# A fused attention and two-MoE kernel on one core: the second block of tokens also multiplied in 256-token pieces in its first half, attention steps spread over three quarter stages

## The chip, the core and the metric

The kernel runs on one core of a Trainium2 chip. A core has five engines that run side by side, each through its own list of instructions in order: TensorE (PE; its weight loads are shown apart as PEld), VectorE (DVE), ScalarE (ACT), GpSimd (POOL) and SyncE (SP), which issues the DMAs here. An instruction that waits holds up all that stand behind it on its engine. The metric is the device time of one execution in microseconds (us); lower is better.

## The reference

Three layers follow one another, all in float32:

```python
# 1. mLSTM attention: batch 2, 8 heads, 768 steps, head size 40
m_new = np.maximum(f_gate[:, :, t] + m, i_gate[:, :, t])
C = f_stab * C + i_stab * outer(v_t, k_t);  n = f_stab * n + i_stab * k_t
y[:, :, t] = sigmoid(o_t) * (C @ q_t) / max(|n . q_t|, 1)
# 2. first MoE: x is [1536, 320], w_in [320, 2048], w_out [2048, 320]
h = x @ w_in
g = np.where(h >= 1, h, np.where(h <= -1, 0.0, (h + 1) ** 2 / 4))
x = g @ w_out
# 3. second MoE: 8 experts, w1[e] [320, 1024], w2[e] [1024, 320]
P = exp(x @ w_gate - max), then 8 rounds of row and column scaling
out = sum over e of P[:, e] * (relu(x @ w1[e]) @ w2[e])
```

## The kernel before, in words

The 1536 tokens are worked as 12 attention tiles of 128 (tile t is chunk t // 2 of batch t % 2; the state `Cst` of a batch is carried from tile t to t + 2). The output of a tile goes, split into a high and a low part, into `XH` and `XL`, which hold all tokens and are the input of the first MoE.

Float32 accuracy is made from pieces: a product of the first MoE takes, for each of its three parts of the 320 inputs, high by high, high by low and low by high, in 8 matmuls (`gemm_k`, L124, into a bank `bk_g1`); the second product takes 8 more (`moe1_g2`, L557 to L561, into three banks `bk_g2`). Between the two stand the activation in `moe1_act`: three passes of ScalarE (L541 to L543), a maximum of VectorE (L545), a copy on ScalarE (L546, the high part) and a subtraction on VectorE (L547, the low part).

The first MoE runs in four stages of 512 tokens, by the table `STAGES` (L40): tokens 0-511 with the first half of d_ff (hf 0) in products of 256 tokens, tokens 512-1023 with both halves in products of 512, tokens 0-511 with the second half, tokens 1024-1535 with both. A bank `bk_g1` holds 512 columns: one block of d_ff for 512 tokens, or two blocks for 256. In the text a "product" is what fills one such bank; there are 8 to each half of d_ff and 512 tokens. With 256-token pieces the stage also begins with three matmuls that set the banks `bk_g2` to zero (L578), and each product with two matmuls of zeros that are overwritten (`warm`, L296). In those pieces the activation is done in place in the bank, which so stays occupied until L547.

Attention is written as a generator (`attn`) whose steps are issued between the products. A tile takes eight such steps: scores (L379) of four heads, a scan along time on VectorE (L383) that makes the decay factors, their product `A` with the scores (L385), the same for the other four heads, the read of the state (L395, into the one bank `bk_ax`), `A` times the values (L400), the state's update (L407, L440), the division and gate (L419 to L433), a transpose (L446) and the split into `XH` and `XL` (L114, L116). Tiles 0 and 1 are done before stage 0. A credit grows by `RATE` with each block of d_ff, and one step is issued for each whole credit (L609 to L620); no step is issued past tile 7 before the fourth block of the second half of stage 1 (L612), since the columns of later tokens in `XH` and `XL` are lent to the activations until then. A piece of 256 or 512 tokens starts only when its tiles are done (L592).

The weights of the first MoE come as 64-bit floats and are decoded on chip in 18 pieces (`decode`, L207 to L223: one pass of ScalarE, four of VectorE, then a split); `pump_w` issues one piece's step. Nine pieces belong to the first half of d_ff, and nine to the second, which are issued one for each product from stage 1 on.

The framework orders the instructions of each engine by their dependencies and the order in which they were issued; `tc.issue_after(x)` puts what is issued under it on the engine of x behind x in that order; it adds no semaphore wait of its own.

Of the kernel before, what the change touches and what calls it, by code (L numbers as in the profile page):

```python
# [34 lines left out]
WA, WG = 4, 2  # L35
PUMP = (0, 2, 4, 5, 6, 7, 10, 12, 13)
GP = 8
RATE = ((3.4, 0), (0, 2.25), (0, 2.25), (2, 2))

STAGES = ((0, (0,), 256), (512, (0, 1), 512), (0, (1,), 512), (1024, (0, 1), 512))  # L40
LAG1, LAG2 = 2, 3


# [5 lines left out]
def mlstm_moe_moe_kernel(  # L49
# [76 lines left out]
    with ExitStack() as atx:  # L126
# [346 lines left out]
        def pump_w():  # L473
            w_state[0] = next(wjobs, 99)
# [62 lines left out]
        dve_at = []  # L537
# [31 lines left out]

        credit = 0  # L570
        held = ap.tile([128, 3, 512], F32, name="held")
        for si, (t0, hfs, w) in enumerate(STAGES):
            nf = 512 // w
            f_last = hfs[-1] * 8 + 7
            pp = [bank("g2") for _ in range(3)]
            if w < 512:
                for p in pp:
                    mm(p, wz, wz[:, 0:1].to_broadcast([128, 512]), start=True, stop=False)  # L578
            prevs = []
            for hf in hfs:  # L580
                if si == 1 and hf == 1:
                    while w_state[0] < 18:
                        pump_w()
                    rtx.close()
                    rtx = ExitStack()
                    open_right(rtx, hp=1, raw=2, gw=1)
                    wgr = pools["gw"].tile([128, 3, NE], F32, name="wgr")
                    wgs = pools["gw"].tile([128, 5, NE], F32R, name="wgs")
                    wg2 = pools["gw"].tile([128, 2, 2, NE], F32R, name="wg2")
                    hearly[0] = -1  # L590
                for o in range(0, 512, w):
                    while len(done) * 128 < t0 + o + w:  # L592
                        next(rest)
                    for ff in range(hf * 8, hf * 8 + 8, nf):
                        need_w(ff + nf - 1)
                        pg = bank("g1")
                        if w < 512:
                            warm(WG, pg)
                        for u in range(nf):
                            fc = (ff + u) % 8 * 128  # L600
                            pe_at = gemm_k(pg[:, u * w : u * w + w], WM[hf][0], slice(fc, fc + 128), slice(t0 + o, t0 + o + w))
                        while len(prevs) >= (LAG2 if w == 512 else LAG1):
                            moe1_g2(*prevs.pop(0))
                        st = ff == hfs[0] * 8 and w == 512
                        sp = ff + nf - 1 == f_last and o + w == 512
                        prevs.append(([p[:, o : o + w] for p in pp], st, sp, ff, w, *moe1_act(pg, w < 512)))
                        if w_state[0] < (9, 18, 18, 18)[si]:
                            pump_w()
                        credit += nf * RATE[si][hf]  # L609
                        while credit >= 1:  # L610

                            if len(done) >= 8 and (si == 0 or si == 1 and ff < 8 + LAG2):  # L612
                                break
                            if si:

                                with tc.issue_after(pe_at[0].ins), tc.issue_after(dve_at[-3].ins):
                                    next(rest, None)
                            else:
                                next(rest, None)
                            credit -= 1  # L620
                        if si == 3 and ff == 11:
                            nc.sync.dma_start(wgr, w_gate)
                            split_k(wgs, 0, NE, wgr)
                            act(out=wg2.rearrange("p k u e -> p u k e"), in_=f(wgs[:, 0:4, :]).rearrange("p (u k) e -> p u k e", u=2), func=ACTF.Copy)
                            cur, jobs = expert_w(0)
                        if si == 3 and ff >= 11:
                            next(jobs, None)
                            next(jobs, None)
            for _ in jobs if si == 3 else ():
                pass  # L630
            for p in prevs:
                moe1_g2(*p)
            if si == 0:
                for k, p in enumerate(pp):
                    act(out=held[:, k, :], in_=p, func=ACTF.Copy)
                continue
            if si == 2:
                for k, p in enumerate(pp):
                    vec.tensor_tensor(out=p, in0=p, in1=held[:, k, :], op=ALU.add)
            tr = htile(512, "gs")  # L640
            act(out=tr[0:64], in_=pp[2][64:128], func=ACTF.Copy)
            act(out=tr[64:128], in_=pp[2][0:64], func=ACTF.Copy)
            vec.tensor_tensor(out=tr, in0=pp[2], in1=tr, op=ALU.add)
            split_x([(0, pp[0]), (1, pp[1]), (2, tr)], slice(t0, t0 + 512))
# [159 lines left out]
```

## Time and profile before

| | us |
|---|---|
| median of 3 runs (lowest to highest) | 995.71 (994.46 to 996.32) |
| the profiled execution: its time | 994.85 |
| the profiled execution: span from first to last instruction | 993.1 |
| stage 0 (tokens 0-511, hf 0), from PE's first product | 36.4 to about 116.5 |
| stage 1, first half (tokens 512-1023, hf 0) | 116.5 to 143.5 |
| stage 1, second half | 143.5 to 196.8 |
| stage 2 (tokens 0-511, hf 1) | 196.8 to 231.2 |
| stage 3 (tokens 1024-1535) | 231.2 to 292.4 |
| second MoE | 292.4 to 993.1 |

The start and end of a row of the timeline are microseconds from the span's start. A busy time of PE is no measure of its work, as matmuls overlap: what one costs in a stream is the distance from its start to the next one's start.

### The profile page before, as it was taken

The page shows a single profiled execution, that of the slowest core. Times are in us where ns is not written, and L with a number is a line of the kernel's source. Part 1 is how long each engine was busy: PE and PEld are TensorE (multiplying, and loading weights), DVE is VectorE, ACT ScalarE, POOL GpSimd, SP SyncE. Part 2 cuts the span into 40 slices and gives each one's busy share as a digit, 9 for nine tenths or more (in the row PEclk, how much of TensorE's full clock was granted, in tenths as well). Part 3 has the DMA queues.
Part 4 walks back from the last instruction along what each step waited for, and adds up shares of the span by engine and source line. Part 5 has one row for each costly group of instructions (what it writes and reads, how often), then busy time and mean ns, then how long its engine had stood idle before and what let it go on. Part 6 is the DMA issues. An engine that isn't in the chain of part 4 may idle for free.

```text
span 993.1 us, 13483 instructions
## 1 busy us (share of the span) xinstructions
PE 979.6 (99%) x5520; PEld 861.8 (87%) x5520; DVE 470.1 (47%) x853; ACT 344.8 (35%) x622; POOL 31.2 (3%) x43
## 2 busy tenths in 40 slices
PE   9999899999999999999999999999999999999998
PEld 5789788887878899999999999989999999999997
DVE  9999977655563644322522432242253234222222
ACT  3743684477773224211411321141132123111111
POOL 2212101000000000000000000000000000000000
PEclk9999999999999999999999999999999999999999
DMA  5865413000132002100400210030021002000000
GB/s 171 263 169 172 143 57 99 12 1 0 47 113 75 1 1 64 54 1 1 117 1 1 74 44 1 7 111 1 1 87 31 1 17 72 1 1 1 27 27 27
DMA packets 42190, 51.91 MB, mean 52 GB/s; under 512 B 3360, under 2 KB 35744, under 8 KB 42128
## 3 DMA queue, kind: packets, MB, share of 16 engines
q1 hardware_dynamic: 42128, 51.05, 17.3%
q8 instruction: 43, 0.70, 0.3%
q14 instruction: 19, 0.16, 0.0%
HBM read 49.03 MB, written 2.01 MB: 51 GB/s over the span
## 4 chain that ended last, share of the span: by engine, by line
PE 89%; DVE 5%; ACT 3%; DMA 1%; issue 1%; SPq 0%; DVEq 0%; ACTq 0%
PE bk_g L124 41%; PE bk_g L704 9%; PE bk_g L706 8%; PE bk_g L705 8%; PE bk_ax L705 3%; PE bk_ax L704 3%; PE bk_ax L706 3%; PE bk_at L400 2%; PE bk_g L296 2%; PE bk_g L559 2%; PE bk_g L558 1%; PE bk_g L557 1%; PE bk_at L379 1%; DMA raw<-in_w_dram 1%; PE bk_g L561 1%
## 5 line engine op out<-in xcount | busy, mean ns | idle before, releaser
L124 PE MATMUL bk_g<-XH,wk 128*128 128x512 f32 (+1 forms) x1240 | 399.8, 388 | 1.6 <-DVE gs L545 1.6
L724 DVE SCALAR_TENSOR_TENSOR lo<-bk_g,hi 128x512 fp32r<-128x512 f32 x192 | 132.6, 691 | 372.6 <-ACT hi L723 371.7
L124 PE MATMUL bk_g<-XL,wk 128*128 128x512 f32 (+1 forms) x744 | 285.4, 384 | 0.0
L723 ACT ACTIVATE hi<-bk_g 128x512 fp32r<-128x512 f32 x192 | 114.9, 599 | 453.2 <-PE bk_g L124 453.0
L124 PEld LDWEIGHTS bk_g<-XH,wk 128*128 128x128 f32 x1240 | 230.6, 188 | 45.1 <-DVE gs L545 2.6
L704 PE MATMUL bk_g<-wf,hi 128*128 128x320 f32 x576 | 177.4, 308 | 1.1 <-ACT hi L723 1.1
L705 PE MATMUL bk_g<-wf,hi 128*128 128x320 f32 x576 | 177.0, 307 | 0.0
L706 PE MATMUL bk_g<-wf,lo 128*128 128x320 f32 x576 | 176.9, 308 | 0.0
L124 PEld LDWEIGHTS bk_g<-XL,wk 128*128 128x128 f32 x744 | 140.0, 188 | 21.4
L704 PEld LDWEIGHTS bk_g<-wf,hi 128*128 128x128 f32 x576 | 108.0, 187 | 8.1 <-ACT hi L723 1.6
L705 PEld LDWEIGHTS bk_g<-wf,hi 128*128 128x128 f32 x576 | 108.1, 188 | 6.3
L706 PEld LDWEIGHTS bk_g<-wf,lo 128*128 128x128 f32 x576 | 107.9, 187 | 0.0
L705 PE MATMUL bk_ax<-wf,hi 128*128 128x320 f32 x192 | 59.1, 308 | 0.0
L704 PE MATMUL bk_ax<-wf,hi 128*128 128x320 f32 x192 | 59.0, 307 | 0.0
L706 PE MATMUL bk_ax<-wf,lo 128*128 128x320 f32 x192 | 58.4, 304 | 0.0
L545 DVE TENSOR_TENSOR gs<-bk_g,gs 128x512 f32<-128x512 f32 x40 | 27.5, 688 | 26.8 <-ACT gs L543 26.4
L541 ACT ACTIVATE gs<-bk_g 128x512 f32<-128x512 f32 x48 | 28.5, 594 | 28.7 <-PE bk_g L124 28.1
L738 DVE SCALAR_TENSOR_TENSOR acc<-bk_g,P,acc 128x320 f32<-128x320 f32 x63 | 30.8, 545 | 15.3 <-PE bk_g L706 15.3
L531 DVE TENSOR_TENSOR wf<-raw,wf 128x640 fp32r<-128x640 f32 x32 | 26.3, 826 | 20.7 <-ACT wf L530 20.5
L704 PEld LDWEIGHTS bk_ax<-wf,hi 128*128 128x128 f32 x192 | 36.1, 188 | 0.0
L706 PEld LDWEIGHTS bk_ax<-wf,lo 128*128 128x128 f32 x192 | 36.1, 188 | 0.0
L705 PEld LDWEIGHTS bk_ax<-wf,hi 128*128 128x128 f32 x192 | 35.9, 187 | 0.0
(198 smaller groups left out, 999.6 us busy)
## 6 DMA issues: line engine op xcount, KB each, us to landing
raw<-in_w_dram SPq DMA_DIRECT2D x32, 320.0 KB
raw<-in_w_dram SPq DMA_DIRECT2D x32, 256.0 KB
kvo_t<-in_kvo_dram SPq DMA_DIRECT2D x12, 484.0 KB
raw<-in_w_out_dram SPq DMA_DIRECT2D x8, 640.0 KB
raw<-in_w_in_dram SPq DMA_DIRECT2D x8, 512.0 KB
raw<-in_w_dram SPq DMA_DIRECT2D x64, 64.0 KB
qk<-in_qk_dram SPq DMA_DIRECT2D x24, 160.0 KB
G<-g_d SPq DMA_DIRECT2D x5, 512.0 KB
```

Of the source, the lines that this page charges most:

```text
L124: return [mm(dst, a, b, start=i == 0, stop=i == len(seq) - 1) for i, (a, b) in enumerate(seq)]
L296: mm(to, wz, wz[:, 0:1].to_broadcast([128, 512]), start=True, stop=True)
L400: mm(pa[:, h * 41 : (h + 1) * 41], A[h % 2][:, h // 2, :], vw[:, h, :], start=True, stop=True)
L531: vec.tensor_tensor(out=wf[:, fs, 320:640], in0=rs[n], in1=f(wf[:, fs, 0:320]), op=ALU.subtract)
L541: act(out=t, in_=pg, func=ACTF.Relu, scale=-1.0, bias=1.0)
L545: dve_at.append(vec.tensor_tensor(out=g, in0=pg, in1=t, op=ALU.max))
L704: mm(pp[i], hi[:, ts], wf[:, ff, 0:320], start=st, stop=False)
L705: mm(pp[i], hi[:, ts], wf[:, ff, 320:640], start=False, stop=False)
L706: mm(pp[i], lo[:, ts], wf[:, ff, 0:320], start=False, stop=sp)
L723: act(out=hi, in_=pg, func=ACTF.Relu)
L724: vec.scalar_tensor_tensor(out=lo, in0=pg, scalar=0.0, in1=f(hi), op0=ALU.max, op1=ALU.subtract)
L738: vec.scalar_tensor_tensor(out=acc[:, t, :], in0=pp[i], scalar=P[:, t, e : e + 1], in1=acc[:, t, :], op0=ALU.mult, op1=ALU.add)
```

## The change

Four edits. The table `STAGES` holds a width for each half of d_ff, and stage 1 has 256 tokens for its first half and 512 for its second. Its banks are therefore zeroed at its start (`zeroed`), and its first eight products carry the two matmuls of zeros. `RATE` gives 2.4 steps for a block in stage 0 (3.4 before) and 2.4 in the first half of stage 1 (none before). From stage 1 on, `pump_w` is issued behind the last-but-one maximum (`dve_at[-2]`). The attention steps of stage 1's first half are issued freely; those of its second half and of later stages stay behind the matmul and the maximum as before.

```diff
-RATE = ((3.4, 0), (0, 2.25), (0, 2.25), (2, 2))
-STAGES = ((0, (0,), 256), (512, (0, 1), 512), (0, (1,), 512), (1024, (0, 1), 512))
+RATE = ((2.4, 0), (2.4, 2.25), (0, 2.25), (2, 2))
+STAGES = ((0, ((0, 256),)), (512, ((0, 256), (1, 512))), (0, ((1, 512),)), (1024, ((0, 512), (1, 512))))
...
-        for si, (t0, hfs, w) in enumerate(STAGES):
-            nf = 512 // w
-            f_last = hfs[-1] * 8 + 7
+        for si, (t0, hfs) in enumerate(STAGES):
+            f_last = hfs[-1][0] * 8 + 7
+            zeroed = hfs[0][1] < 512
...
-            if w < 512:
+            if zeroed:
                 for p in pp:
                     mm(p, wz, wz[:, 0:1].to_broadcast([128, 512]), start=True, stop=False)
...
-            for hf in hfs:
+            for hf, w in hfs:
+                nf = 512 // w
...
-                        st = ff == hfs[0] * 8 and w == 512
+                        st = ff == hfs[0][0] * 8 and not zeroed
...
                         if w_state[0] < (9, 18, 18, 18)[si]:
-                            pump_w()
+                            if si:
+                                with tc.issue_after(dve_at[-2].ins):
+                                    pump_w()
+                            else:
+                                pump_w()
                         credit += nf * RATE[si][hf]
...
-                            if si:
+                            if si and hf + si > 1:
```

How the instructions of an engine stand is shown at three places. The first is PE in the first half of stage 1, for one product and the start of what follows it. Before (`bk_g1_1390` is the bank of the product, `wk_88` its weights):

```order
L124 MATMUL bk_g1_1390<-XH_66,wk_88 128x512
L124 MATMUL bk_g1_1390<-XL_67,wk_88 128x512
L124 MATMUL bk_g1_1390<-XH_66,wk_88 128x512 x2
L124 MATMUL bk_g1_1390<-XL_67,wk_88 128x512
L124 MATMUL bk_g1_1390<-XH_66,wk_88 128x512 x2
L124 MATMUL bk_g1_1390<-XL_67,wk_88 128x512
L561 MATMUL bk_g2_1268<-XL_67,wf_89 128x512
```

And in the changed kernel, from the two matmuls of zeros on (`bk_g1_1457` is the bank):

```order
L296 LDWEIGHTS wz_91
L296 MATMUL bk_g1_1457<-wz_91 128x512
L296 LDWEIGHTS wz_91
L296 MATMUL bk_g1_1457<-wz_91 128x512
L124 MATMUL bk_g1_1457<-XH_66,wk_88 128x256
L124 MATMUL bk_g1_1457<-XL_67,wk_88 128x256
L124 MATMUL bk_g1_1457<-XH_66,wk_88 128x256 x2
L124 MATMUL bk_g1_1457<-XL_67,wk_88 128x256
L124 MATMUL bk_g1_1457<-XH_66,wk_88 128x256 x2
L124 MATMUL bk_g1_1457<-XL_67,wk_88 128x256
```

Eight matmuls of 512 columns became 16 of 256, with two matmuls of zeros ahead of them.

The second place is DVE in stage 0, around the second product `A` of tile 4 (`A_752` before, `A_846` after; `G0_90` holds its decay factors, `g_all_80` those of the next tile). Before:

```order
L385 TENSOR_TENSOR A_744<-bk_at_739,G0_90 128x512
L433 TENSOR_TENSOR sg_637<-sg_637,den_717 128x320
L383 SCALAR_TENSOR_TENSOR G0_90<-G0_90,id4_116 128x512
L213 TENSOR_SCALAR dv_757<-dv_757 128x512
L385 TENSOR_TENSOR A_752<-bk_at_747,G0_90 128x512
L116 TENSOR_TENSOR XL_67<-bk_ax_727,XH_66 128x3x128
L214 TENSOR_SCALAR dv_757<-dv_757 128x512
```

After:

```order
L545 TENSOR_TENSOR bk_g1_735<-bk_g1_735,gs_770 128x512
L440 TENSOR_TENSOR Cst_114<-bk_at_708,Cst_114 40x4x41 x2
L383 SCALAR_TENSOR_TENSOR G0_90<-G0_90,id4_116 128x512
L547 TENSOR_TENSOR XL_67<-bk_g1_735,XH_66 128x512
L116 TENSOR_TENSOR XL_67<-bk_ax_779,XH_66 128x3x128
L385 TENSOR_TENSOR A_796<-bk_at_791,G0_90 128x512
L383 SCALAR_TENSOR_TENSOR G0_90<-G0_90,id4_116 128x512
L383 SCALAR_TENSOR_TENSOR g_all_80<-g_all_80,id4_116 128x512
L385 TENSOR_TENSOR A_846<-bk_at_799,G0_90 128x512
```

The activation of the fourth product (bank 735, L545 and L547), the split L116 of the tile before and the next tile's first scan now stand ahead of the second product `A` of tile 4.

The third place is PE in the second half of stage 1 and after. Before, a late tile (tile 10, scores in `bk_at_1791`) stands with whole products between its steps:

```order
L379 MATMUL bk_at_1791<-qk0_94 128x128 x4
L124 MATMUL bk_g1_1796<-XH_66,wk_654 128x512
L124 MATMUL bk_g1_1796<-XL_67,wk_654 128x512
L124 MATMUL bk_g1_1796<-XH_66,wk_654 128x512 x2
L124 MATMUL bk_g1_1796<-XL_67,wk_654 128x512
L124 MATMUL bk_g1_1796<-XH_66,wk_654 128x512 x2
L446 MATMUL bk_ax_1753<-cst_64,sg_1732 128x128 x3
L124 MATMUL bk_g1_1796<-XL_67,wk_654 128x512
L557 MATMUL bk_g2_1266<-hi_1603,wf_655 128x512
```

After (from tile 8's update of the state to tile 9's `A` times values; the product is in `bk_g1_2010`):

```order
L407 MATMUL bk_at_1817<-vw_1333,kw_115 104x82 x4
L124 MATMUL bk_g1_2010<-XL_67,wk_622 128x512
L124 MATMUL bk_g1_2010<-XH_66,wk_622 128x512
L379 MATMUL bk_at_1848<-qk1_95 128x128 x4
L124 MATMUL bk_g1_2010<-XH_66,wk_622 128x512
L379 MATMUL bk_at_1856<-qk1_95 128x128 x4
L400 MATMUL bk_at_1870<-vw_1832,A_1853 128x41
L124 MATMUL bk_g1_2010<-XL_67,wk_622 128x512
L446 MATMUL bk_ax_1836<-cst_64,sg_1815 128x128 x3
L124 MATMUL bk_g1_2010<-XH_66,wk_622 128x512 x2
L400 MATMUL bk_at_1870<-vw_1832,A_1861 128x41
```

The steps of tiles 8 to 11 follow one another with single matmuls of a product between them: all four tiles stand within the last four products of stage 1, and none is left for stage 2.

## Rows read from the trace of the kernel before

**Rows 1.** The page's head and its busy times by engine.

```profile
span 993.1 us, 13483 instructions
...
PE 979.6 (99%) x5520; PEld 861.8 (87%) x5520; DVE 470.1 (47%) x853; ACT 344.8 (35%) x622; POOL 31.2 (3%) x43
```

**Rows 2.** Stretches: length, busy us (instructions) by engine, PE clock, DMA.

```profile
36.40:116.50 80.10, 75.64 (x589) 68.78 (x587) 75.24 (x146) 38.36 (x76) 19.45 (x20) 0.98 0.63 187
116.50:143.50 27.00, 25.55 (x119) 21.02 (x119) 25.14 (x48) 24.61 (x48) 0.00 (x0) 1.00 0.29 92
143.50:196.80 53.30, 51.84 (x299) 44.16 (x298) 35.17 (x61) 24.76 (x46) 4.76 (x6) 1.00 0.17 52
```

**Rows 3.** PE timeline, stage 0: start, length, instruction, [idle before].

```profile
62.34 0.28 PE L557 MATMUL bk_g<-XH,wf 128*128 128x256 f32 x1
...
64.14 0.28 PE L561 MATMUL bk_g<-XL,wf 128*128 128x256 f32 x1
66.33 0.50 PE L557 MATMUL bk_g<-XH,wf 128*128 128x256 f32 x2 [1.92 <-ACT XH L546]
```

**Rows 4.** PE timeline, first half of stage 1: two second products' first matmuls.

```profile
134.44 0.39 PE L557 MATMUL bk_g<-XH,wf 128*128 128x512 f32 x1
...
138.07 0.39 PE L557 MATMUL bk_g<-XH,wf 128*128 128x512 f32 x1
```

**Rows 5.** The chain of waits: start, length, what (matmuls of zeros).

```profile
19.19 2.61 PE bk_g L296 x12
```

**Rows 6.** DVE timeline, stage 0, up to tile 4's second product `A`.

```profile
63.40 0.41 DVE L214 TENSOR_SCALAR dv<-dv 128x512 int32<-128x512 int32 x1
63.74 0.69 DVE L545 TENSOR_TENSOR bk_g<-bk_g,gs 128x512 f32<-128x512 f32 x1
64.34 0.68 DVE L217 SCALAR_TENSOR_TENSOR dv<-raw,dv 128x512 int32<-128x512 int32 x1
...
69.17 1.22 DVE L383 TENSOR_TENSOR_SCAN G<-G,id 128x512 f32<-128x512 f32 x1
70.30 0.18 DVE L430 RECIPROCAL den<-den 128x8 f32<-128x8 f32 x1
...
73.57 0.69 DVE L385 TENSOR_TENSOR A<-bk_at,G 128x512 f32<-128x512 f32 x1
74.17 0.55 DVE L116 TENSOR_TENSOR XL<-bk_ax,XH 128x384 fp32r<-128x384 f32 x1
74.63 0.65 DVE L214 TENSOR_SCALAR dv<-dv 128x512 int32<-128x512 int32 x1
```

**Rows 7.** PE timeline: stage 0's first product, tile 4's L400, stage 0's end.

```profile
36.38 0.41 PE L124 MATMUL bk_g<-XH,wk 128*128 128x256 f32 x1
...
74.31 1.76 PE L400 MATMUL bk_at<-vw,A 128*128 128x41 f32 x14
...
119.03 0.40 PE L124 MATMUL bk_g<-XL,wk 128*128 128x512 f32 x1
```

**Rows 8.** PE timeline: later waits of stage 0 and of stage 1's start.

```profile
101.40 0.41 PE L446 MATMUL bk_ax<-cst,sg 128*128 128x128 f32 x2 [0.53 <-DVE sg L433]
...
123.37 0.50 PE L124 MATMUL bk_g<-XH,wk 128*128 128x512 f32 x1 [1.43 <-DVE gs L545]
```

**Rows 9.** PE timeline: tile 8 in a dense place, tile 10 in a loose one.

```profile
158.07 1.95 PE L379 MATMUL bk_at<-qk 104*128 104x128 f32 x16
159.85 1.02 PE L395 MATMUL bk_ax<-Cst,qk 104*128 104x82 f32 x8
161.97 0.39 PE L400 MATMUL bk_at<-vw,A 128*128 128x41 f32 x2 [1.10 <-DVE A L385]
...
184.46 1.02 PE L395 MATMUL bk_ax<-Cst,qk 104*128 104x82 f32 x8
185.31 1.92 PE L400 MATMUL bk_at<-vw,A 128*128 128x41 f32 x16
```

**Rows 10.** A stretch right after the wait at 66.33, columns as in Rows 2.

```profile
68.00:70.00 2.00, 2.00 (x11) 1.96 (x10) 1.94 (x6) 0.00 (x0) 0.00 (x0) 0.50 1.03 304
```

## The prediction, made before the changed kernel ran

> **What bounds the kernel now.** I read the page's busy times first, then the windows by stage, then PE's timeline, and last DVE's timeline where PE waits. The page has PE busy for 99% of the span [rows 1]; since matmuls overlap, that says only that no other engine is near. The starts say more. In stage 0 sixteen matmuls of 256 columns go from 62.34 to 64.14 in 15 steps, 0.12 us each [rows 3]. In stage 1 a whole product with its second product, 16 matmuls of 512, takes 138.07 - 134.44 = 3.63 us, 0.227 each [rows 4]. Twelve matmuls of zeros take 2.61, 0.2175 each [rows 5]. An attention matmul costs 0.11 (the 16 scores from 158.07 to 159.85) [rows 9].
>
> With these I count what PE loses. From its first product at 36.38 to 119.03 [rows 7] its order holds 256 matmuls of 256 columns (30.7 us), 39 of zeros (8.5), 306 of attention (33.7) and 4 of 512 (0.9): 73.8 of 82.65 us, so 8.9 are lost. A wait for the maximum L545 at 123.37 [rows 8] adds 1.6: 10.5 us until then. The reader is to see in the windows what the loss comes from: DVE is busy 75.2 of the 80.1 us of stage 0, and in the first half of stage 1 DVE and ScalarE are both at 25 of 27; in the second half DVE is at 35 of 53 and PE runs nearly dry of waits [rows 2]. So stage 0 is carried by DVE as much as by PE.
>
> The clearest proof is tile 4. Its second product `A` starts on DVE at 73.57 and takes 0.69, to 74.26 [rows 6]; PE's L400, which reads it, starts at 74.31 [rows 7]. DVE ahead of this is dense. PE had by then 113 matmuls of 256, 21 of zeros and 120 of attention, 13.6 + 4.6 + 13.2 = 31.3 of 37.9 us: 6.6 lost. The rest, 3.9, is lost later, in waits like that at 101.40 and 123.37 [rows 8].
>
> **The change part by part.** *Narrow products.* In the first half of stage 1 each of 8 products (16 matmuls of 512, 3.63) becomes 32 of 256 and two of zeros, 3.84 + 0.435 = 4.275: 0.645 more, 5.2 for the eight. Three zeroing matmuls add 0.65. Together +5.8 us of PE work. It is hidden only where PE would wait anyway, and its place is late: in the changed order DVE has 95.5 us of work from stage 0's start to the end of this half, by the durations of the profile, and PE 103.5, so PE is the longer one there. I take all of it. If waits hid it: 0.
>
> The Trainium skill bears on this price (TensorE: Matmul & The Clock Gate, Back-to-back issue gap): an isolated warm matmul spaces by N / 2.4 + 2.5 ns, 109 ns for 256 columns and 216 for 512, so that halving would cost only 2.7 ns a pair. The rows here show 120 and 227, 13 ns a pair. By the page the eight products would cost 3.8 instead of 5.2, and the forecast below would be 1000.6.
>
> *Fewer steps in stage 0.* At 4.8 credits for a product (6.8 before), only tiles 2 to 6 stay in stage 0 and tile 7 moves into the first half of stage 1. That should ease DVE, but the order shows where it does not. Ahead of the second product `A` of tile 4 stand 76 DVE instructions from the start of stage 0, where 68 stood. The eight are one each of L116 (0.46), L214 (0.34), L217, L220, L236, L545, L547 (0.60 each) and the scan L383 (1.13), by starts [rows 6]: 4.9 us. Ahead of PE's L400 there are 16 + 2 more matmuls of 256, 2 of zeros and 8 of attention: 3.5 us. PE meets the same wait with 1.4 less cover: 6.6 + 1.4 = 8.0 lost by tile 4. Behind it DVE is no longer ahead in need: for tile 5's second `A`, DVE's order holds 47.3 us, and PE's 48.9 (before: 45.9 and 43.4). So from there I leave only waits within a chain, like those at 101.40, and the new zeroing matmuls, which need the copies of the three banks that close stage 0: 1.5 us, where before 3.9 were lost. Sum 9.5 against 10.5: -1.0. Bounds: 4.7 if DVE had neither its idle moments nor its slow instructions, such as the L214 of 0.65 against 0.41 [rows 6], which gives -5.8; and 11.9 if as much is lost after tile 4 as before, +1.4.
>
> *Later decoding.* Its nine pieces stay in the same half and change place on DVE and ScalarE, and their loads on SP, where they now stand between the loads of tiles 8 and 9. Each narrow product has about 4.25 us of DVE work beside 4.275 of PE, and its bank is free only after L547; between a product's end and the start of the second-next one PE has another product, two second products and zeros, 3 x 1.92 + 0.435 = 6.2 us, and the chain of six instructions from L541 to L547, 0.6 to 0.7 each [rows 6], takes some 4.5 with its hand-overs (an estimate). I take 0; if each of the eight were late by 0.5, +4.
>
> *The late tiles.* Credits are counted in the first half of stage 1 as well, while steps stop at tile 7: 16 products give 76.8 credits for 48 steps. At the fourth block of the second half, 28.8 + 9 = 37.8 are open, more than the 32 steps of tiles 8 to 11. Before, some 15 were open, two tiles' worth. So all four tiles go in one train within four products, as the order shows. What that costs is in tile 8 before: scores, state read and L400 directly behind one another. PE is ready at 159.85 + 8 x 0.11 = 160.74 and starts at 161.97, 1.2 lost to scan and `A`; tile 10, with products between, starts L400 right after its L395 (185.31 - 184.46 = 0.85 for eight) [rows 9]. Tile 8 keeps its wait. Tiles 9, 10 and 11 have at most two matmuls, 0.45, between their last scores and L400: 3 x 1.2 less 0.45 = 3.2, where tile 9 before lost about 0.8: +2.4. Bounds: -2.3 if the train had no waits at all (what tiles 8 and 9 lose now), +7 if every tile lost 2.3 and the loads of tiles 10 and 11, which wait for tiles 8 and 9 to be read, came late as well.
>
> *Sum.* 5.8 - 1.0 + 0 + 2.4 = +7.2 on the profiled execution's own time, 994.85: 1002.0 us. Its time lies 0.9 under the median of the runs shown, 995.71, and within their 994.46 to 996.32, so I leave the sum as it is.
>
> **Rivals.** A, faster: DVE lets go of stage 0. For it: DVE has 5 tiles instead of 6 there, and loses part of its 75 us. Against it: the count at tile 4. If only the 1.5 us of chain waits were left of 10.5 and the train cost nothing more: 5.8 - 9.0 = -3.2, 991.7. It decides once under about 2.7 us are lost up to the end of the first half of stage 1.
>
> B, no change: the loss falls by half of what A says and the train costs nothing more, 5.8 - 4.5 = +1.3, 996.2. For it: the train's DVE work (about 35 us, counted in its order) is a little less than PE's (four products of 3.63 and 4 x 51 attention matmuls, 37). Against: the wait at 161.97 comes with DVE far from full.
>
> C, slower still: the train is held by its chain and its loads, +7 instead of +2.4: 1006.6. For it: each tile's state, bank `bk_ax` and buffers are handed on to the next but one.
>
> D: PE's clock. After the 1.92 us of idle at 66.33 [rows 3] the granted clock was 0.50, the lower level of 1.2 GHz, through 68 to 70 us [rows 10]. In the changed order the last 12 us of PE work ahead of tile 4's L400 take some 18 us with their waits. At 1.2 GHz all along they would take 24: 6 more, 1008.0. Against it: one such stretch in the whole kernel before. The Trainium skill says of this (same page, HAM oscillation) that waits between groups of matmuls can throw the clock back each time; the trace has it once.
>
> **How the numbers follow.** Forecast 0.52 (its own range 999 to 1005), A 0.10, B 0.14, C 0.14, D 0.10. Below 996 lie A and part of B, above 1009 a part of C and D and the sum of several: the range is 996 to 1009. What 0.2% is here, 2 us, is about what a measurement can tell. Faster 0.10 (A), same 0.14 (B), slower 0.76.
>
> **What would show it.** In the profile after: first products of stage 1 at 4.25 to 4.3 us each instead of 3.63; the second `A` of tile 4 some 5 us later than 73.57 from the same start, and L400 right behind it; no wait like that at 123.37; tiles 8 to 11 in one stretch of some 38 to 42 us with PE waits on `A` at L400; stages 2 and 3 shorter or the same, the second MoE unchanged at 700 us. It is wrong if the wait at tile 4 is gone, if the narrow products overlap waits that I do not see, or if the second MoE moves.

## The result, and the profile after

The changed kernel takes 1008.6 us (median of 4 runs, 1008.0 to 1009.22) against 995.89 for the kernel before in the same rounds (994.46 to 996.32): ratio 1.0133, 95% interval 1.0118 to 1.0148, so 12.7 us slower. The forecast was 1002.0, +7.2 on the profiled execution and +6.1 on this median: the right side, and the range of 996 to 1009 just holds the result, but only about half of the change.

The page's head, which answers to [rows 1]:

```profile
span 1007.1 us, 13767 instructions
...
PE 989.7 (98%) x5667; PEld 874.1 (87%) x5667; DVE 471.1 (47%) x853; ACT 346.5 (34%) x622; POOL 33.9 (3%) x43
```

The span is 14.0 us longer. From the first product's first matmul to the last second product of the first MoE the trace has 269.96 us where it had 255.78; from there to the last matmul 697.39 where it had 697.35. So all of it lies in the first MoE, as forecast. I use that length, "first MoE", for every kernel below: it leaves out what the second MoE does in one execution or another.

The windows by stage, answering to [rows 2], with the same columns (stage 0, first half of stage 1, then the 53.3 us after it):

```profile
36.30:116.60 80.30, 72.47 (x545) 65.71 (x543) 68.86 (x130) 34.38 (x68) 20.49 (x18) 0.94 0.57 171
116.60:155.40 38.80, 38.21 (x303) 35.55 (x303) 32.12 (x62) 30.33 (x56) 1.47 (x2) 1.00 0.25 81
155.40:208.70 53.30, 51.27 (x328) 45.53 (x327) 38.24 (x70) 24.13 (x46) 4.97 (x6) 0.97 0.22 65
```

Stage 0 is as long as before (80.3 against 80.1 us) with one tile of attention less in it, and PE and DVE are both less busy. That is where most of the forecast's error lies. The timeline of PE there, answering to [rows 3, 7]:

```profile
60.76 0.28 PE L561 MATMUL bk_g<-XL,wf 128*128 128x256 f32 x1
62.73 0.76 PE L557 MATMUL bk_g<-XH,wf 128*128 128x256 f32 x2 [1.69 <-ACT XH L546]
63.29 0.41 PE L560 MATMUL bk_g<-XH,wf 128*128 128x256 f32 x1
64.69 1.01 PE L296 MATMUL bk_g<-wz 128*128 128x512 bf16 x2 [0.99 <-DVE XL L547]
...
74.90 0.78 PE L446 MATMUL bk_ax<-cst,sg 128*128 128x128 f32 x3 [1.46 <-DVE sg L433]
76.17 1.79 PE L379 MATMUL bk_at<-qk 104*128 104x128 f32 x8 [0.49 <-DVE Cst L440]
...
83.17 1.09 PE L400 MATMUL bk_at<-vw,A 128*128 128x41 f32 x9
```

And DVE's, answering to [rows 6]:

```profile
67.61 0.68 DVE L236 TENSOR_TENSOR wk<-raw,wk 128x512 fp32r<-128x512 f32 x1
71.19 0.50 DVE L423 TENSOR_TENSOR hv<-hv,bk_at 128x328 f32<-128x328 f32 x1 [2.90 <-PE bk_at L400]
...
81.22 0.67 DVE L385 TENSOR_TENSOR A<-bk_at,G 128x512 f32<-128x512 f32 x1
```

The reader is to see a circle. PE reaches the third product's second product early, since less attention stands ahead of it, and waits for its activation (62.73, 64.69); the kernel before has this wait too (1.92 us at 66.33 [rows 3]). Then DVE waits 2.9 us for PE's L400 of tile 3. Then PE waits for DVE's `sg` at 74.90 and for its `Cst` at 76.17. Behind the first and the last of these waits PE works at half clock; the windows, columns as in [rows 10], show two such stretches in stage 0 and a third in tile 8, where before only 67.1 to 70.6 us was slow:

```profile
62.80:69.63 6.83, 5.84 (x21) 4.32 (x22) 5.49 (x10) 1.67 (x3) 0.74 (x1) 0.50 0.58 176
69.63:76.45 6.82, 4.86 (x40) 4.26 (x40) 5.22 (x13) 1.97 (x5) 0.74 (x1) 1.00 0.66 216
76.45:79.87 3.42, 3.42 (x16) 2.96 (x15) 3.39 (x5) 0.74 (x3) 0.00 (x0) 0.50 0.02 5
...
175.44:178.85 3.41, 3.41 (x17) 3.22 (x17) 2.10 (x6) 0.00 (x0) 1.29 (x2) 0.50 0.42 127
```

0.50 is the lower level, 1.2 GHz, and 1.00 is 2.4. Two narrow products' first second-product matmuls, answering to [rows 4], are 4.28 us apart, where 3.63 was:

```profile
140.68 0.28 PE L557 MATMUL bk_g<-XH,wf 128*128 128x256 f32 x1
...
144.96 0.28 PE L557 MATMUL bk_g<-XH,wf 128*128 128x256 f32 x1
```

Last, PE in tile 8, answering to [rows 9], and a wait in stage 2 that the kernel before does not have:

```profile
170.49 1.02 PE L395 MATMUL bk_ax<-Cst,qk 104*128 104x82 f32 x8
173.35 0.39 PE L400 MATMUL bk_at<-vw,A 128*128 128x41 f32 x2 [1.84 <-DVE A L385]
...
219.16 0.50 PE L124 MATMUL bk_g<-XH,wk 128*128 128x512 f32 x1 [1.30 <-DVE gs L545]
```

Counted as in the prediction (starts against the price of each matmul, from stage 0's first product on), PE has 5.8 us more work. Up to the end of the first half of stage 1 it loses 15.3 us where before it lost 10.7 (+4.6; the prediction's 10.5 stopped at 123.37). In the second half of stage 1 it loses 5.0 against 2.8 (+2.2), and in stage 2, where the wait at 219.16 is, 2.1 against 0.6 (+1.5). That makes 14.1 of the 14.2.

### The profile page after: what moved, and what is told of

Read it like the earlier page. It is cut to its first block, busy times and chain, and to the rows that moved or that the text cites. A ratio compares the mean times of both kernels' runs of the same rounds, so it can differ in the third digit from the quotient of the medians.

```text
span 1007.1 us, 13767 instructions
## 1 busy us (share of the span) xinstructions
PE 989.7 (98%) x5667; PEld 874.1 (87%) x5667; DVE 471.1 (47%) x853; ACT 346.5 (34%) x622; POOL 33.9 (3%) x43
## 4 chain that ended last, share of the span: by engine, by line
PE 88%; DVE 7%; ACT 2%; issue 2%; DMA 1%; POOL 0%; SPq 0%; DVEq 0%; ACTq 0%; POOLq 0%
PE bk_g L124 41%; PE bk_g L711 8%; PE bk_g L709 8%; PE bk_g L710 8%; PE bk_ax L710 3%; PE bk_ax L709 3%; PE bk_ax L711 3%; PE bk_g L558 2%; PE bk_g L559 2%; PE bk_g L557 2%; PE bk_at L400 2%; PE bk_g L296 1%; PE bk_at L379 1%; DMA raw<-in_w_dram 1%; PE bk_g L561 1%
## 5 line engine op out<-in xcount | busy, mean ns | idle before, releaser
L124 PE MATMUL bk_g<-XH,wk 128*128 128x512 f32 (+1 forms) x1280 | 405.0, 383 | 1.5 <-DVE gs L545 1.5
L124 PE MATMUL bk_g<-XL,wk 128*128 128x512 f32 (+1 forms) x768 | 289.5, 378 | 0.0
L124 PEld LDWEIGHTS bk_g<-XH,wk 128*128 128x128 f32 x1280 | 236.7, 189 | 44.8 <-DVE gs L545 2.5
L124 PEld LDWEIGHTS bk_g<-XL,wk 128*128 128x128 f32 x768 | 145.0, 189 | 20.9
L743 DVE SCALAR_TENSOR_TENSOR acc<-bk_g,P,acc 128x320 f32<-128x320 f32 x63 | 30.8, 545 | 15.3 <-PE bk_g L711 15.3
L296 PE MATMUL bk_g<-wz 128*128 128x512 bf16 x114 | 32.5, 409 | 2.5 <-DVE XL L547 1.5
```

The costliest lines, as they stand in the source:

```text
L124: return [mm(dst, a, b, start=i == 0, stop=i == len(seq) - 1) for i, (a, b) in enumerate(seq)]
L296: mm(to, wz, wz[:, 0:1].to_broadcast([128, 512]), start=True, stop=True)
L743: vec.scalar_tensor_tensor(out=acc[:, t, :], in0=pp[i], scalar=P[:, t, e : e + 1], in1=acc[:, t, :], op0=ALU.mult, op1=ALU.add)
```

## The experiments

Theory: the excess over the forecast sits in stage 0, in the circle of waits and the clock that falls in it, with smaller shares at tile 8 and at 219 us. Rivals: DVE's order alone, the narrow products, or the tied decoding. The table has each run's median and the ratio to the kernel before in its own rounds; from the profiled execution the first MoE's length, the start of the first matmul that needs tile 4's second `A`, counted from stage 0's first product ("tile 4"; before 37.9, changed kernel 47.0), and the mean granted clock over 62 to 82 us.

| kernel | median us | ratio (95%) | first MoE | tile 4 | clock 62-82 |
|---|---|---|---|---|---|
| before | 995.89 | | 255.8 | 37.9 | 0.91 |
| changed | 1008.6 | 1.0133 (1.0118-1.0148) | 270.0 | 47.0 | 0.74 |
| 1 before, 2.4 credits | 1006.1 | 1.0095 (1.0073-1.0117) | 269.0 | 48.8 | 0.77 |
| 2 changed, 3.4 credits | 1002.81 | 1.0063 (1.0043-1.0083) | 264.0 | 38.0 | 0.91 |
| 3 credits cut | 1007.51 | 1.0115 (1.0085-1.0146) | 267.1 | 46.3 | 0.83 |
| 4 zeros in the waits | 1008.13 | 1.0120 (1.0097-1.0144) | 267.8 | 44.2 | 1.00 |
| 5 no zeros in stage 1 | 1003.59 | 1.0069 (1.0050-1.0087) | 264.8 | 47.1 | 0.66 |
| 6 decoding untied | 1009.69 | 1.0137 (1.0117-1.0157) | 271.8 | 47.1 | 0.74 |
| 7 before, zeros in the wait | 997.54 | 1.0013 (0.9998-1.0028) | 255.6 | 37.3 | 1.00 |
| 8 zeros at tile 8 | 1009.29 | 1.0131 (1.0111-1.0151) | 268.9 | 45.1 | 0.91 |
| 9 edits of 3, 4, 5 | 998.44 | 1.0029 (1.0018-1.0039) | 260.6 | 44.5 | 1.00 |
| 10 four remainders left out | 1002.5 | 1.0071 (1.0058-1.0083) | 265.9 | 41.0 | 0.91 |
| 11 before, no zeros in stage 0 | 997.38 | 1.0017 (1.0001-1.0033) | 256.5 | 37.9 | 0.83 |
| 12 changed, 3.4, no zeros | 999.65 | 1.0040 (1.0027-1.0052) | 262.4 | 40.5 | 0.91 |

The intervals are some 2 to 6 us wide. Executions of one kernel differ, and their times go with the clock granted to them: the kernel before took 994.1 us at a mean of 1.0 and 1000.1 at 0.993 in the rounds of experiments 5 to 8. So one to three microseconds are read from the traces, and only larger differences from the medians. But a trace is one execution: the same steps of stage 0 took up to 2 us more in one than in another (experiment 4), so such readings are made place by place.

**Experiment 1: the kernel before with one number of the change.**

```
-RATE = ((3.4, 0), (0, 2.25), ...
+RATE = ((2.4, 0), (0, 2.25), ...
```

> The kernel before with one number changed: 2.4 credits a hidden block in stage 0 instead of 3.4. Stage 1 keeps its 512-token products, so tile 7 is done in one piece ahead of them. Theory (the loss sits in stage 0: with fewer attention steps between the products PE's waits come closer together, the clock falls to its lower level twice, and DVE in turn waits for PE): the same waits as in the changed kernel, about 3.5 us ahead of the third product's second product and 3.6 us around tile 3's transposes, half clock near 63 to 70 us and 76 to 80 us, some 12 us lost by tile 4's L400 (8.3 less than that in the kernel before is wrong then), and a time of 1000 to 1004 us, with 1.5 to 3 of it from tile 7 standing alone. Rival (stage 0 costs no more than before and the excess over the forecast comes from the narrow products and the decoding among them): 994 to 998 us, about 8 us lost by tile 4's L400.

Measured: 1006.1 us, outside both ranges. Up to tile 4 it is much like the changed kernel: the same waits, two stretches at half clock, and tile 4 at 48.8 (1.2 of the 1.8 us more are there at tile 2's L400 already). So the circle needs no narrow product. But the time says less than I meant it to, for tile 7 alone ahead of stage 1 costs far more than the 1.5 to 3 us I had put on it: four waits of 1.1, 3.1, 0.6 and 2.2 us, and half clock behind them.

```profile
62.00:82.00 20.00, 15.01 (x82) 12.26 (x81) 17.72 (x32) 5.73 (x12) 3.99 (x5) 0.77 0.44 143
120.00:138.00 18.00, 11.32 (x56) 8.71 (x55) 15.94 (x34) 8.46 (x18) 1.52 (x2) 0.81 0.37 120
```

**Experiment 2: the changed kernel with the old credits.**

```
-RATE = ((2.4, 0), (2.4, 2.25), ...
+RATE = ((3.4, 0), (0, 2.25), ...
```

> The changed kernel with the credits of the kernel before (3.4 in stage 0, none in the first half of stage 1): all tiles up to 7 are done in stage 0, the narrow products of stage 1 stand by themselves, the decoding stays tied, and no credits pile up. Theory: stage 0 as in the kernel before, half clock in one stretch only, 10 to 11 us lost up to the end of the first half of stage 1, and the price of narrow products as forecast: 995.9 + 5.8 less up to 1.6 for the wait before the maximum that vanishes, 1000 to 1002.5 us. Rival (narrow products or the tied decoding bring waits of their own): 1005 us or more, with waits between the narrow products.

Measured: +6.3 us by the ratio, 1002.81 by the median, 0.3 above the theory's range and under the rival's. Tile 4 is back at 38.0 and no wait stands among the narrow products after the first. What is over 5.8 comes behind tile 8: there the clock falls, although PE's wait there is 0.89 us, shorter than the 1.10 of the kernel before [rows 9]. The windows of stage 0's middle and of tile 8:

```profile
62.00:82.00 20.00, 17.81 (x132) 16.56 (x132) 19.17 (x42) 9.16 (x18) 2.64 (x3) 0.91 0.59 164
168.00:182.00 14.00, 13.78 (x84) 12.87 (x85) 8.06 (x16) 2.97 (x7) 2.03 (x4) 0.76 0.44 134
```

So narrow products and tied decoding account for about half of the 12.7, and the credits for the other half.

**Experiment 3: the credits cut.**

```
                 if si == 1 and hf == 1:
+                    credit = min(credit, 6)
```

> The changed kernel with the credits cut to 6 where the second half of stage 1 begins, so that at its fourth product 15 are open as in the kernel before, and tiles 8 to 11 are spread again over stages 1 and 2. Theory: the train costs the 1.9 us that PE loses more in 168 to 205 us and the 1.5 us wait at 219 us: 1005 to 1006.7 us, with no half clock near 175 us. Rival (what the train saves later, it pays back: the same attention has to be done anyway): 1008 to 1009.5 us.

Measured: the profiled execution took 1005.2 us, in the theory's range; the median, 1007.51, is not, and its interval holds the changed kernel's ratio. The trace decides one part: the wait at 219 us is gone, with PE busy all through stage 2 (30.00 of 30).

```profile
62.00:66.00 4.00, 1.95 (x10) 1.26 (x11) 4.00 (x8) 2.40 (x4) 0.01 (x1) 0.95 0.15 40
...
174.00:178.00 4.00, 4.00 (x23) 3.81 (x23) 2.18 (x7) 0.00 (x0) 1.29 (x2) 0.61 0.47 140
...
200.00:230.00 30.00, 30.00 (x155) 25.15 (x154) 17.15 (x32) 20.23 (x36) 0.00 (x0) 1.00 0.00 1
```

The other part of the theory falls: the clock still falls at 174 to 178 us, and the wait for tile 8's `A` is still 1.83 us. With the tiles spread again, PE loses 4.5 us in the second half of stage 1 instead of 5.0. So the train itself costs about 0.5, and the rest belongs to tile 8's start. The first MoE is 2.8 us shorter, but 0.7 of it is gained in stage 0, whose steps are the same: its clock was better in this execution (tile 4 at 46.3).

**Experiment 4: zeros in the two waits of stage 0.**

```
+    for _ in range({(0, 4): 28, (0, 6): 24}.get((prevs[0][7], prevs[0][3]), 0) if si == 0 else 0):
+        mm(prevs[0][0][0], wz, wz[:, 0:1].to_broadcast([128, w]), start=False, stop=False)
-    moe1_g2(*prevs.pop(0))
+    moe1_g2(*prevs.pop(0)[:7])
...
```

> The changed kernel with 52 matmuls of zeros (256 columns, added into the bank that the second product writes anyway), 28 ahead of the third product's second product and 24 ahead of the fourth's, on PE just where it waits in stage 0. Nothing else moves. Theory (the clock): the granted clock stays at 1.0 between 62 and 80 us, the work behind the two waits runs at full speed, DVE waits less for PE at tile 3, and the time falls by 3 to 5 us to 1003.5 to 1005.5 us, although PE does 5.6 us of work more. Rival (DVE's order alone sets when tile 4 is done): the same time or up to 2 us more, 1008 to 1011 us, with the same start of tile 4's L400.

Measured: 1008.13 us; the median does not tell it from the changed kernel, so the 3 to 5 us are not there. PE, DVE, and the windows of the changed kernel and of this one:

```profile
61.56 3.28 PE L605 MATMUL bk_g<-wz 128*128 128x256 bf16 x28
...
71.98 1.39 PE L605 MATMUL bk_g<-wz 128*128 128x256 bf16 x11
73.59 0.44 PE L446 MATMUL bk_ax<-cst,sg 128*128 128x128 f32 x2 [0.22 <-DVE sg L433]
...
80.84 1.43 PE L400 MATMUL bk_at<-vw,A 128*128 128x41 f32 x12
```

```profile
69.88 0.50 DVE L423 TENSOR_TENSOR hv<-hv,bk_at 128x328 f32<-128x328 f32 x1 [0.91 <-PE bk_at L400]
```

```profile
62.00:82.00 20.00, 16.32 (x92) 13.74 (x92) 17.03 (x32) 5.46 (x11) 3.02 (x4) 0.74 0.43 134
62.00:82.00 20.00, 19.13 (x154) 16.30 (x152) 19.01 (x34) 7.45 (x16) 5.26 (x5) 1.00 0.49 144
```

The clock stays at 1.00, DVE works 19.0 of these 20 us instead of 17.0, and tile 4 comes at 44.2 instead of 47.0, although 5.7 us of matmuls were added; the first MoE is 2.2 us shorter. So the theory holds in kind and for about half its size. Without any edit to stage 0 the same is seen: the changed kernel and experiments 3, 5, 6 and 8 have the same steps there and line up by the clock that the one profiled execution of each got. Tile 4 comes at 47.1 with 0.66, at 47.0 and 47.1 with 0.74, at 46.3 with 0.83 and at 45.1 with 0.91; with the zeros at 44.2 with 1.00. DVE's wait for PE's L400 of tile 3 goes along: 4.16, 2.90 and 2.95, 2.18, 1.93, and 0.91 us with the zeros. So half clock lengthens the circle, but 0.91 us of this wait is left at full clock.

**Experiment 5: no zeros ahead of stage 1's narrow products.**

```
-                        if w < 512:
+                        if si == 0:
                             warm(WG, pg)
```

> The changed kernel without the two zero matmuls ahead of each of the eight narrow products of stage 1 (those of stage 0 stay). Theory (the first half of stage 1 is bound by PE, so each zero matmul there is paid in full): 16 x 0.2175 = 3.5 us less, 1005.1 us, within 1004 to 1006, and full clock from 117 to 155 us all the same. Rival (they fill waits for the activations, or keep the clock up): no gain, waits of the same size in their place or a stretch at the lower clock level there, 1007.5 to 1010 us.

Measured: 1003.59 us, 5.0 less and 0.4 under the theory's range; 5.2 less in the first MoE. By the time that PE is ready for tile 8's L400, 3.2 of the zeros' 3.5 are gained, with full clock in that half. The other 2.0 come at tile 8, whose `A` then is late by 0.72 instead of 1.84, with no slow stretch behind it; how the zeros make that `A` late was not tried.

```profile
118.00:155.00 37.00, 36.46 (x295) 35.39 (x295) 32.35 (x63) 29.58 (x57) 2.06 (x2) 1.00 0.24 75
```

```profile
169.32 0.39 PE L400 MATMUL bk_at<-vw,A 128*128 128x41 f32 x2 [0.72 <-DVE A L385]
```

**Experiment 6: the decoding untied.**

```
-                            if si:
-                                with tc.issue_after(dve_at[-2].ins):
-                                    pump_w()
-                            else:
-                                pump_w()
+                            pump_w()
```

> The changed kernel with the decoding not tied to the maximum of the product before last (nothing else undone). Theory (the tie costs nothing, as forecast, since PE is the longer engine there): 1007.6 to 1009.6 us, with the same waits up to 117 us and tile 8's L400 late by the same 2 us. Rival (the tie pushes DVE's decoding to where tile 8 needs DVE, and so makes the 2 us wait at tile 8 and the fall of the clock behind it): 1005 to 1007 us, and that wait at 1.2 us or less as in the kernel before.

Measured: 1009.69 us, 0.1 above the theory's range and nowhere near the rival's. The wait at tile 8 is 1.55 us, and a longer slow stretch follows it:

```profile
172.00:183.00 11.00, 11.00 (x52) 10.30 (x52) 4.73 (x13) 0.90 (x3) 1.68 (x2) 0.53 0.34 109
```

The tie costs nothing that these runs can tell.

**Experiment 7: zeros in the wait of the kernel before.**

```
+    for _ in range(22 if si == 0 and (prevs[0][7], prevs[0][3]) == (0, 4) else 0):
+        mm(prevs[0][0][0], wz, wz[:, 0:1].to_broadcast([128, w]), start=False, stop=False)
-    moe1_g2(*prevs.pop(0))
+    moe1_g2(*prevs.pop(0)[:7])
...
```

> The kernel before with 22 matmuls of zeros (2.4 us, added into the bank that the second product writes anyway) where PE waits 2.6 us ahead of the third product's second product, before its one stretch at half clock (67 to 70.6 us). Theory (a wait is followed by the lower clock, and the slow work behind it is lost): the stretch is gone, 1 to 2 us less, 993.5 to 995 us. Rival (DVE sets tile 4, the slow PE work lies beside it): no change or up to 1 us more, 995 to 997 us.

Measured: 997.54 us, 0.5 above the rival's range, and by the ratio no difference (1.0013, 0.9998 to 1.0028); the theory is out. The windows of the kernel before and of this one:

```profile
62.00:82.00 20.00, 17.80 (x131) 16.32 (x131) 19.14 (x42) 9.65 (x19) 2.63 (x3) 0.91 0.61 172
62.00:82.00 20.00, 19.31 (x159) 17.68 (x159) 19.76 (x43) 9.90 (x19) 2.63 (x3) 1.00 0.65 180
```

The slow stretch is gone, tile 4 comes 0.6 us earlier, and the first MoE is the same (255.6 against 255.8): DVE is busy 19.76 of 20 us, and was busy 19.14 with the slow stretch, so it sets the pace. That is the difference from experiment 4, where DVE stood 2.9 us for PE: a slow PE costs only where DVE waits for it.

**Experiment 8: zeros in tile 8's wait.**

```
-            if 2 <= t < 8:
-                warm(WA, pa)
+            if 2 <= t < 9:
+                warm(WA if t < 8 else 8, pa)
```

> The changed kernel with eight zero matmuls (1.74 us) ahead of tile 8's L400, in the wait of 1.96 us at 171.4 to 173.4 us. Theory (the clock falls behind that wait, from 175.4 to 178.9 us, and the train loses 1.7 us by it): full clock there, and 1 to 2 us less, 1006.6 to 1007.6 us. Rival (the train is held by its chain of scan, A and L400, whatever the clock): 1008.3 to 1009.5 us, with the waits behind tile 8 as before.

Measured: 1009.29 us, with an interval that tells nothing; the profiled execution took 1007.41. My edit missed its place: the zeros write the bank that the first `A` frees, so they too start only when it is there (171.88), not in the wait. The window of tile 8 has full clock all the same.

```profile
171.88 1.90 PE L296 MATMUL bk_at<-wz 128*128 128x512 bf16 x8 [1.74 <-DVE A L385]
```

```profile
168.00:182.00 14.00, 11.82 (x92) 10.32 (x91) 9.37 (x19) 4.11 (x8) 2.16 (x3) 1.00 0.34 100
```

Its first MoE is 1.0 us shorter, but it also had a better clock in stage 0, where it is the changed kernel (tile 4 at 45.1), so by its time this experiment is inconclusive. Taken by itself, the second half of stage 1 has 0.8 us less lost and 1.7 us of zeros more.

**Experiment 9: the edits of 3, 4 and 5 together.**

> Three of the earlier edits of the changed kernel at once: the 52 matmuls of zeros in stage 0's two waits, the credits cut to 6 before the second half of stage 1, and no zero matmuls ahead of the narrow products of stage 1. Stage 0 keeps its 2.4 credits. Theory (the parts are separate places and add up): from the profiled executions 2.4 for the first (1008.95 to 1006.57), 2.6 for the second (1.1 in the train, 1.45 at 219 us) and 5.1 for the third (1008.95 to 1003.81): 998.9 us, within 998 to 1000.5, with full clock to 240 us. Rival (they remove the same loss, so that the clock or DVE gives it back): 1001.5 us or more.

Measured: 998.44 us, ratio 1.0029 (1.0018 to 1.0039), as the theory says. In the first MoE 2.8, 2.2 and 5.2 add up to 10.2, and 9.4 was measured; the 0.7 that experiment 3 gained in stage 0 stands in this sum twice, as the zeros gain it as well. Its windows from stage 0 to the end of stage 3 have no slow stretch at all:

```profile
36.30:115.30 79.00, 74.05 (x599) 67.69 (x598) 68.47 (x130) 34.88 (x69) 20.03 (x18) 1.00 0.59 177
115.30:300.00 184.70, 182.38 (x1034) 156.71 (x1034) 122.20 (x212) 127.68 (x230) 7.01 (x8) 1.00 0.18 54
```

Its interval lies clear of that of experiment 5 (1.0050 to 1.0087). So what each of 3 and 4 could not show by its median, the two show together: about 0.4%, 4 us.

**Experiment 10: less work for DVE ahead of tile 4.**

```
-def moe1_act(pg, early):
+def moe1_act(pg, early, skip=False):
...
     act(out=hi, in_=g, func=ACTF.Copy)
+    if skip:
+        return hi, hi
...
+    prevs.append((..., *moe1_act(pg, w < 512, si == 0 and o == 0)))
```

> The changed kernel where the first four products of stage 0 leave out the remainder (the subtraction L547 on DVE, 0.6 us each) and the second products read the rounded part in its place, so that the remainder's share of these is not computed; PE does as many matmuls as before, in an order that the scheduler shifts. Theory (what is left of stage 0's loss when the clock is kept up is DVE's work ahead of tile 4's second A): 2.4 us less DVE work there, L400 of tile 4 2.4 to 4 us earlier than 83.2, 1004.5 to 1006.5 us. Rival (PE's own waits for the activations and the transposes set it, DVE is not the bound): L400 of tile 4 within 1 us of 83.2, 1007.5 to 1009.5 us.

Measured: 1002.5 us, 2 us below the theory's range. L400 of tile 4 starts at 77.17, 6 us earlier, for 2.4 us of DVE work:

```profile
77.17 1.87 PE L400 MATMUL bk_at<-vw,A 128*128 128x41 f32 x16
```

The scheduler also placed PE's work anew, and the clock over 62 to 82 us is 0.91, as in the kernel before, so the 6 us are not all DVE's: against experiment 8, at 0.91 too, 4.1 are left. The rival's figure is out, but how much of the 4.1 is DVE's and how much comes of PE's new order is not shown. The count of the prediction less 2.4 is 40.4, and 41.0 was measured; with PE's own order (experiment 8) that count is 2.3 short at the same clock, 42.8 against 45.1, so that the near hit is partly luck.

**Experiment 11: the kernel before without stage 0's zeros.**

```
-                            warm(WG, pg)
+                            pass
```

> The kernel before without the two zero matmuls ahead of each product of stage 0 (16 in all, 3.5 us of PE). Theory (stage 0 is carried by DVE, where PE waits 10.5 us anyway, so zeros there cost little): 994.5 to 996.5 us, within 0.2% of the kernel before. Rival (they cost in full, as in stage 1): 991.5 to 993 us. Should the clock need them: one more stretch at half clock in 40 to 100 us and 997 us or more.

Measured: 997.38 us (ratio 1.0017, 1.0001 to 1.0033); the profiled execution took 995.04. The rival, 3.5 us less, is out, and so is the theory, by 0.9 us; the third case came, 997 us or more and one more stretch at half clock (77.14 to 80.55 us, beside 66.90 to 70.31):

```profile
62.00:82.00 20.00, 16.64 (x110) 15.52 (x109) 18.94 (x41) 6.58 (x13) 2.62 (x3) 0.83 0.61 174
```

In the trace 3.0 us of PE work are gone from the first MoE (two of the 16 matmuls stand ahead of it), and it is 0.7 longer. The same two zero matmuls cost nearly all of their length in stage 1 (experiment 5), and to leave them out gains nothing here. Whether that is because DVE sets the pace, or because the zeros spare a slow stretch, one trace doesn't tell.

**Experiment 12: narrow products alone, without their zeros.**

> The changed kernel with the credits of the kernel before (3.4 in stage 0, none in the first half of stage 1) and without the zero matmuls ahead of stage 1's narrow products: only the halved matmuls and three zeroing ones are left of the narrow half. Theory: 5.2 - 3.5 + 0.65 = 2.4 us more PE work than in the kernel before, 998 to 999.5 us. Rival (narrow products bring more than their matmuls, as the 6.9 us of the run with the zeros against 5.8 hints): 1000 us or more.

It has the edits of 2 and 5. Measured: 999.65 us, between the two ranges; +4.0 by the ratio where 2.4 of work was added. In the trace PE loses 4.6 us more than in the kernel before up to the end of the narrow half. Of this 2.1 lie in stage 0, where this execution had one more slow stretch (47.1 to 50.5 us; tile 4 at 40.5, against 38.0 in experiment 2 with the same steps), and 2.5 in the narrow half, in a wait for its first product's activation and slow work behind it:

```profile
127.20 0.50 PE L557 MATMUL bk_g<-XH,wf 128*128 128x256 f32 x2 [2.06 <-ACT XH L546]
```

```profile
126.00:134.00 8.00, 6.61 (x40) 6.43 (x41) 7.56 (x14) 6.62 (x12) 0.00 (x0) 0.79 0.22 68
```

Every kernel with narrow products is slower than the kernel before, by 0.29% at the least (experiment 9), and none of the three edits to the kernel before is faster than it.

## Why the prediction was right or wrong

*Narrow products, +5.8:* right. 4.28 us each against 4.275 forecast, no wait above 0.4 us among them behind 117.6 us, and nearly all of the zeros in them paid (3.2 of 3.5, experiment 5). By the isolated spacing that the Trainium skill states (TensorE: Matmul & The Clock Gate, Back-to-back issue gap) the eight products would, as an estimate, have cost 3.8 us more; they cost 8 x 0.65 = 5.2 more, by the pitch of 0.12 that stage 0 had shown [rows 3]. (The prediction's 2.7 ns a pair is a slip: by the formula that the Trainium skill gives there it is 2.5, and the 3.8 goes by that.)

*Fewer steps in stage 0, -1.0:* this step failed. PE lost 4.6 us more there instead of 1.0 less, outside the bound of +1.4 that I gave. Up to tile 4 the forecast was 42.8 us from the first product (37.9 + 4.9); it took 47.0. I counted DVE's instructions ahead of tile 4's second `A` and let PE arrive with less cover. I did not ask what PE would do with the cover gone at places before: it met two waits of 2.7 and 2.0 us on DVE's and ScalarE's chain, the first of them as in the kernel before, the clock fell to its lower level behind each, and then DVE, which in my count never waits, stood 2.9 us for PE.

Two things were left out, then, and they are about equal. With the clock at 1.00 in both kernels (experiments 4 and 7) tile 4 comes at 44.2 and 37.3, 6.9 apart; at 0.91 in both (experiment 8 and the kernel before) at 45.1 and 37.9, 7.2 apart; 4.9 was forecast. So 2.0 to 2.3 of the excess of 4.2 are there at either clock: the count was short, and DVE and PE wait for each other, 0.91 us at L423 even at full clock. I can't divide this part further. The rest, about 2, goes with the clock, which I had put at nothing in the sum. Behind tile 4 I had put 1.5 us of loss; it was 3.2, of which one wait of 1.5 us for tile 5's `sg` at 104.60 stands untouched in experiment 4 as well. What makes `sg` late there was not tried.

*Later decoding, 0:* right (experiment 6).

*Late tiles, +2.4:* the size was near (+2.2 in the second half of stage 1), but by luck, as the mechanism was wrong. I let tiles 9, 10 and 11 each wait for `A`; in the train PE waits 0.19 us in all at their L400s. What costs is the start of tile 8, whose `A` is late by 1.84 us instead of 1.10, and the slow stretch of 3.4 us behind it. Both go when stage 1's zeros go, and with the same train PE then loses 2.9 us in that half against 2.8 in the kernel before (experiment 5); spreading the tiles gains about 0.5 (experiment 3). And I missed what stage 2 does with its attention gone: it loses 1.5 us more, in a wait for the maximum at its third product. The kernel before had attention there, and with the credits cut the wait is gone (experiment 3).

*The rivals.* D had the right kind of cause with 10% on it: more of the first MoE's work at half clock, 13.7 us in three stretches against 3.4 in one. I argued against it that the trace before has it once. That one stretch cost nothing there (experiment 7) because DVE was busy all along, so it told nothing of the price elsewhere. But that D's 1008.0 lies near the 1008.6 measured is luck: it put 6 us of clock ahead of tile 4, where about 2 are shown. The Trainium skill has a like case (same page, A second HAM failure mode: psum-queue depth-cycling): the engine idles briefly and often between groups of matmuls, and the clock swings between its two levels. The trace agrees in part: half clock stands at or behind the waits of 1.7 and 1.0, 1.5 and 0.5, and 1.8 us, but not behind those of 1.5 us at 104.60 and 1.3 us at 219.16. A and B are out, as the loss in stage 0 grew; C's train did not cost its 7 us.

*The signs named in advance.* Products of 4.28, no wait like that of 123.37, stages 2 and 3 no longer than before, and the second MoE unchanged at 697.4 us came as said. Tile 4's second `A` came 7.7 us later in place of 5, and L400 1.3 us behind its end, not right behind: PE was late there, not DVE. The late tiles took some 36.5 us (168.7 to 205.2) in place of 38 to 42, without the waits at L400 behind tile 8.

## What to carry to other kernels

Where two engines hand work to each other several times in a stage, counting one engine's instructions up to one hand-over is not enough: walk through every earlier one, and when work that covered a wait moves away, put the wait itself, the clock behind it and the other engine's answering wait into the sum. A size that comes out right is no proof of its term: look for the waits that the term was made of. A filler matmul cost nothing that could be measured in stage 0, which VectorE paces (experiments 7 and 11), and nearly its full length in the half that TensorE paces (experiment 5), so it is to be placed in waits, not with every product. A counter that goes on running while its work is held back moves that work in a lump, and its cost is looked for in the stage that the work has left, too.

## What the runs showed of the hardware

Half clock is not a fixed price. 3.4 us of it cost the kernel before nothing (255.8 against 255.6 us without it), since DVE was busy beside it. In the changed kernel the same steps of stage 0 brought tile 4 at 45.1, 46.3, 47.0 and 47.1 us as the mean granted clock over 62 to 82 us was 0.91, 0.83, 0.74 and 0.66.

After much the same wait at tile 8 (1.10 us before, 0.89 in experiment 2) the clock stayed at 1.00 in the one kernel and fell to a mean of 0.76 over 168 to 182 us in the other. What decides it I can't say from these runs.

The time of an execution goes with its mean granted clock, also for one and the same kernel. Experiment 9 took 998.03 to 998.86 us in its six executions at 1.0, and 999.97 and 1000.0 in the two at 0.998; experiment 7 took 994.72 to 995.08 in the three at 0.999 or 1.0, and 996.63 to 999.9 in the nine at 0.995 to 0.998.
